# First loads in halves, one weight piece later in the queue, and signs folded into other operations, in a retention and feed-forward kernel

## The chip, the cores and the metric

The kernel runs on one core of a Trainium2 chip. The metric is the device time of one execution in microseconds. Engines are named as in the profile: PE (TensorE; PEld is its weight load), DVE (VectorE), ACT (ScalarE), POOL (GpSimd) and SP (SyncE, whose queue issues the loads and stores; SPq).

## The reference, cut to what matters

Three stages follow each other. Retention over 4 batches, 8 heads, 576 tokens and head size 64; a product of two projections with two more matrices behind it; and a projection with a leaky activation whose slopes are alpha. Inputs of the later stages are float64 weights.

```
scores = q @ k.T / sqrt(64)                 # q, k, v: (4, 8, 576, 64)
ret    = scores * gamma[h] ** (i - j)       # for i >= j, else 0
x      = (ret @ v) as (2304, 512)
h      = ((x @ w1) * (x @ w2)) @ w3         # w1, w2: (512, 1024)
x      = h @ w_out                          # (2304, 512)
g      = max(x @ w_in, 0) + alpha * min(x @ w_in, 0)     # alpha: (2048,)
out    = g @ w_out2                         # (2304, 512)
```

## The kernel before

**Retention** (class Retention) works on chunks of 128 tokens, four and a half of them in a batch, and on pairs of heads; a batch has 4 pairs. For chunk c, `scores(c)` multiplies k and q on PE (L419; L408 for the last, half chunk) and has DVE multiply by the mask into rt (L423, L411); `moments(c)` multiplies k and v (L434) and has DVE and POOL build the running state (L440 to L446); `values(c)` multiplies the state of the chunk before by q (L467) and v by rt (L476), and ACT and DVE split the result into a high and a low part for the next product (L181, L182). q is scaled first by POOL (`scale`, L396 for the 512 full columns and L398 for the 64 last), k by ACT (`prep`, L389, one instruction for each head). A batch is stepped by `steps()`: scores and moments of the next chunk around values of this one.

Batch 0 is done in two halves, r0 (pairs 0 and 1) and r1 (pairs 2 and 3). Ahead of it, `busy(26)` lets PE run 26 matmuls on zeros (L575), and each of r0's first steps ends with one more (`keep_busy`). `ready(2)` and `ready(3)` scale and prepare one pair of r1 each.

**Weights** come in pieces of 512 KB as float64 bits (raw) and are turned into two float32r halves in four steps: `_first` (ACT, L93 and L94), `_second` (DVE, L103 to L108), `_third` (ACT, L114), `_fourth` (DVE, L122). `tick` moves each step by one piece; it also loads ahead, `self.near` pieces beyond the one begun. Pieces 0 and 1 are needed by the first unit of the first product (`ab_unit(0, 0)`), pieces 2 and 3 by the next.

**The first product** is made in units (`ab_unit`, PE L188: 12 matmuls for each half), with retention of batch 1, 2 and 3 put between them a step at a time by `cycle`. A half's result is copied by ACT (L651), multiplied by DVE (L641), split by ACT and DVE (L637, L633) and stored (L630). After the first half of the first unit, `cycle` first ticks the weights (which runs `_third` of piece 2 and then `_first` of piece 3), then flushes what is waiting (L651), then runs the first step of batch 1: scaling and preparing its pairs 0 and 1.

**The order of the loads.** PE, SP and ACT work in the order of the program; DVE's and POOL's order is made by the scheduler from its own estimates. The loads stand in SP's queue as: the row constants, the table (mask, its tail, and the scale of q) of pairs 0 and 1, then q and k, then kv of pairs 0 and 1; weight piece 0; the same for pairs 2 and 3; pieces 1 to 3; pairs 2 and 3 of batch 1 in room of their own (`load_apart`); piece 4; pairs 0 and 1 of batch 1; piece 5 and on.

**The operands of the last product** (class Operands) are made from w_out2 in pairs of pieces x, y, five pairs between 120 and 212 us (the case without `small`) and three later, with `small`, on POOL. For each, `signed` multiplies both pieces by the signs sg of alpha (L309 on DVE; L307 on POOL), `less` makes sums and differences (L290), and `hi` and `lo` split them (L271 on ACT, L275 on DVE).

Of the kernel before, what the change touches and what calls it, by code (L numbers as in the profile page):

```python
# [32 lines left out]
def _f32(ap):  # L33
    return ap.bitcast(F32)
# [112 lines left out]
def retention_moe_kernel(ctx: ExitStack, tc, qk, kv, w_out1, w3t, w12, w_in, w_out2, alpha, c_row, c_pair, out):  # L147
# [11 lines left out]


    al = const.tile([P, 96], F32, name="al")
    al, sg, sal = (al[:, n * C2:(n + 1) * C2] for n in range(3))
    const_r = pool(ctx, "const_r", side="right")
    const_r.tile([P, 120], F32, name="pad")

# [61 lines left out]
    class Operands:  # L227
# [40 lines left out]
        def hi(self, j, u, src):  # L268
            self.u[j, u] = self.places(j, u)
            for h, _, x in self.halves(j, u, src):  # L270
                nc.scalar.copy(h, x)  # L271

        def lo(self, j, u, src):
            for h, l, x in self.halves(j, u, src):
                nc.vector.tensor_tensor(out=l, in0=x, in1=_f32(h), op=ALU.subtract)  # L275
            t = self.u.pop((j, u))
            if j != self.stays:
                for n, op in enumerate(self.PLACES[u]):
                    nc.sync.dma_start(out=wod[WOPS.index(op)][:, j].rearrange("p (h w) -> p h w", h=2),
                                      in_=_f32(t[:, n]))  # L280

        def add(self, j, at, steps, ahead=None):


            w, x, y = self.w, 2 * j, 2 * j + 1
            lower, upper = slice(0, 256), slice(256, 512)
            t = {}

            def less(out, a, b):
                (nc.gpsimd if self.small else nc.vector).tensor_tensor(out=out, in0=a, in1=b, op=ALU.subtract)  # L290

            def sums1():
                a, b = w.ab[x][0], w.ab[y][0]
                t[1] = tmp.tile([P, 512], I32, tag="b", name=f"t1_{j}", bufs=2).bitcast(F32)
                less(t[1][:, lower], a[:, upper], a[:, lower])
                less(t[1][:, upper], b[:, upper], t[1][:, lower])

            def sums3():
                a, b = w.ab[x][0], w.ab[y][0]
                t[3] = tmp.tile([P, 512], I32, tag="b", name=f"t3_{j}", bufs=2).bitcast(F32)  # L300
                less(t[3][:, lower], b[:, upper], a[:, upper])
                less(t[3][:, upper], b[:, lower], t[1][:, upper])

            def signed(i):
                a = w.ab[i][0]
                if self.small:
                    nc.gpsimd.tensor_tensor(out=a, in0=a, in1=sg[:, i:i + 1].to_broadcast([P, 512]), op=ALU.mult)  # L307
                else:
                    nc.vector.tensor_scalar(out=a, in0=a, scalar1=sg[:, i:i + 1], scalar2=None, op0=ALU.mult)  # L309

            parts = {
                "gx": lambda: signed(x), "gy": lambda: signed(y),
                "fx": lambda: w._first(x), "fy": lambda: w._first(y),
                "sx": lambda: w._second(x), "sy": lambda: w._second(y),
                "h1": lambda: self.hi(j, "u1", w.ab[x][0][:, lower]),
                "l1": lambda: self.lo(j, "u1", w.ab[x][0][:, lower]),
                "h2": lambda: self.hi(j, "u2", w.ab[y][0]), "l2": lambda: self.lo(j, "u2", w.ab[y][0]),
                "t1": sums1, "t3": sums3,
                "h3": lambda: self.hi(j, "u3", t[1]), "l3": lambda: self.lo(j, "u3", t[1]),
                "h4": lambda: self.hi(j, "u4", t[3]), "l4": lambda: self.lo(j, "u4", t[3]),  # L320
                "x": lambda: self.load(x + 2), "y": lambda: self.load(y + 2),
            }
# [48 lines left out]
    class Retention:  # L371
# [20 lines left out]
        def scale(self, pairs=None):  # L392
            for p in pairs or self.pairs:
                q, by = qt[self.b][p], qs[:, p]
                full = q[:, 0:512].rearrange("p (c i) -> p c i", i=CH)
                nc.gpsimd.tensor_tensor(out=full, in0=full, in1=by.unsqueeze(1).to_broadcast([P, 4, CH]),  # L396
                                        op=ALU.mult)
                nc.gpsimd.tensor_tensor(out=q[:, 512:S], in0=q[:, 512:S], in1=by[:, 0:64], op=ALU.mult)  # L398

        def scores(self, c):  # L400
            b, n = self.b, self.n
# [168 lines left out]
    load_apart(1, 3, 13)  # L570
    warm = pool(first, "ps_warm", space=PSUM).tile([P, 512], F32, name="warm")
# [8 lines left out]
    r0.scale()  # L580
    r0.prep()

    def keep_busy(step):
        def run():
            step()
            flush()
            busy(1)
        return run

    def ready(p):  # L590
        def run():
            r1.scale([p])
            r1.prep([p])
# [896 lines left out]
```

## Time and profile before

| | |
|---|---|
| median of 3 runs | 780.6 us (779.77 to 782.58) |
| profiled execution | 783.55 us |
| its span, first to last instruction | 781.7 us |
| mean granted clock of PE | 0.997 |
| PE busy | 768.9 us, 98% |
| DVE busy | 587.3 us, 75% |
| ACT busy | 380.4 us, 49% |
| POOL busy | 63.8 us, 8% |

The profile comes from one execution. PE is busy nearly throughout, so the places where it isn't are to be looked for one by one; a busy share is a mean over stages that differ.

### The profile page before, as it was taken

Reading aid. Unit: us, or ns where it says so; the run is one execution under the profiler, and the core shown is the slowest. Engines: PE = TensorE matmul, PEld = TensorE weight load, DVE = VectorE, ACT = ScalarE, POOL = GpSimd, SP = SyncE. Lnnn points to the kernel's source line nnn. Section 1 sums busy time; section 2 is a strip of 40 time slices with the busy share of each in tenths; the row PEclk is TensorE's granted clock in tenths of the full one; section 3 lists DMA queues with packets and bytes.
Section 4 is the critical chain, followed back from the end, with each engine's and each line's share of the span. In section 5 each row is a group of like instructions: output and inputs, shape, how many; then the busy total and the mean of one; then the engine's idle time right before and its main releaser. Section 6 shows DMA issues by size and latency. Waiting matters only on the chain.

```text
span 781.7 us, 13197 instructions
## 1 busy us (share of the span) xinstructions
PE 768.9 (98%) x4928; PEld 688.9 (88%) x4928; DVE 587.3 (75%) x951; ACT 380.4 (49%) x665; POOL 63.8 (8%) x73
## 2 busy tenths in 40 slices
PE   8999999998999999999999999999999999999998
PEld 5788788887788988899999999999999888888887
DVE  4894889569857779688974768778767877777874
ACT  3643474334445466464654546546534444444442
POOL 4410400051000000000000200110200000000000
PEclk9999999999999999999999999999999999999999
DMA  9943965798576667799993796564899754444440
GB/s 353 358 160 105 340 246 202 239 287 259 212 249 204 189 197 256 248 327 368 407 375 138 262 362 225 172 228 154 286 339 366 234 152 128 140 126 136 135 128 28
DMA packets 116225, 182.11 MB, mean 233 GB/s; under 512 B 9920, under 2 KB 82624, under 8 KB 116160
## 3 DMA queue, kind: packets, MB, share of 16 engines
q1 hardware_dynamic: 116160, 181.26, 68.1%
q8 instruction: 39, 0.64, 0.4%
q14 instruction: 26, 0.21, 0.1%
HBM read 117.00 MB, written 64.23 MB: 232 GB/s over the span
## 4 chain that ended last, share of the span: by engine, by line
PE 83%; DVE 7%; DMA 5%; issue 2%; SPq 2%; ACT 1%; POOL 0%; DVEq 0%; ACTq 0%; POOLq 0%
PE h L1063 21%; PE ps L188 19%; PE y L1007 13%; PE o L1208 12%; PE o L1210 6%; PE pw L822 6%; DMA abd<-ab 2%; PE sc L419 2%; PE o L476 2%; DMA cells<-gd 2%; DVE cells L1189 2%; PE o L467 1%; SPq L514 1%; PE st L434 1%; DVE a L108 1%
## 5 line engine op out<-in xcount | busy, mean ns | idle before, releaser
L188 PE MATMUL ps<-xh,w 128*128 128x512 f32 (+1 forms) x640 | 186.1, 372 | 1.8 <-ACT f L651 1.8
L188 PEld LDWEIGHTS ps<-xh,w 128*128 128x128 f32 x640 | 116.1, 188 | 23.3 <-ACT f L651 2.2
L1208 PE MATMUL o<-wop,cells 128*128 128x512 f32 x504 | 126.4, 393 | 0.9 <-DVE cells L1220 0.9
L188 PE MATMUL ps<-xl,w 128*128 128x512 f32 (+1 forms) x320 | 118.0, 369 | 0.0
L1208 PEld LDWEIGHTS o<-wop,cells 128*128 128x128 f32 x504 | 90.8, 189 | 17.7 <-issue 1.4
L1007 PE MATMUL y<-yab,wp 128*128 128x384 f32 x576 | 100.0, 334 | 0.0
L1007 PEld LDWEIGHTS y<-yab,wp 128*128 128x128 f32 x576 | 99.9, 188 | 0.1
L1189 DVE TENSOR_TENSOR cells<-cells,cells 128x1024 fp32r<-128x1024 f32 x63 | 76.4, 1222 | 25.7 <-ACT cells L1183 25.6
L1210 PEld LDWEIGHTS o<-wop,cells 128*128 128x128 f32 x504 | 68.7, 190 | 4.9
L1210 PE MATMUL o<-wop,cells 128*128 128x256 f32 x504 | 70.2, 282 | 0.0
L188 PEld LDWEIGHTS ps<-xl,w 128*128 128x128 f32 x320 | 60.4, 189 | 9.5
L1183 ACT CAST cells<-cells 128x1024 fp32r<-128x1024 f32 x63 | 64.9, 1054 | 7.0 <-DVE cells L1176 4.6
L108 DVE CUSTOM_DVE_ANT_0 a<-a,b 128x1024 uint16<-128x1024 uint16 x72 | 53.2, 738 | 2.9
L1063 PE MATMUL h<-xT,wu 128*128 128x384 f32 x288 | 54.7, 334 | 0.2 <-DVE g L1082 0.2
L1063 PE MATMUL h<-xT,wv 128*128 128x384 f32 x288 | 54.9, 335 | 0.0
L1076 DVE SCALAR_TENSOR_TENSOR g<-h,al,g 128x384 f32<-128x384 f32 x48 | 29.4, 614 | 32.6 <-ACT g L1075 29.5
L637 ACT CAST ab<-f 128x512 fp32r<-128x512 f32 (+1 forms) x40 | 23.1, 577 | 61.2 <-DVE f L641 51.8
L1063 PEld LDWEIGHTS h<-xT,wu 128*128 128x128 f32 x288 | 50.3, 188 | 0.5 <-DVE g L1082 0.5
L1063 PEld LDWEIGHTS h<-xT,wv 128*128 128x128 f32 x288 | 50.3, 188 | 0.3 <-DVE g L1082 0.3
L103 DVE TENSOR_SCALAR a<-a 128x512 f32<-128x512 f32 x72 | 31.9, 443 | 22.9 <-ACT a L93 22.5
L822 PE MATMUL pw<-wo,w 128*128 128x512 f32 x192 | 43.7, 389 | 0.0
L822 PEld LDWEIGHTS pw<-wo,w 128*128 128x128 f32 x192 | 36.0, 188 | 7.4
(130 smaller groups left out, 1139.4 us busy)
## 6 DMA issues: line engine op xcount, KB each, us to landing
gd<-g SPq DMA_DIRECT2D x96, 192.0 KB, 4.4
cells<-gd SPq DMA_DIRECT2D x36, 512.0 KB, 6.3
abd<-ab SPq DMA_DIRECT2D x32, 512.0 KB, 5.2
wod<-wo2u SPq DMA_DIRECT2D x49, 256.0 KB, 4.0
wop<-wod SPq DMA_DIRECT2D x21, 512.0 KB, 6.5
yab<-abd SPq DMA_DIRECT2D x24, 384.0 KB, 8.0
raw<-in_w_dram SPq DMA_DIRECT2D x16, 512.0 KB, 8.0
rawo<-in_w_out_dram SPq DMA_DIRECT2D x16, 512.0 KB, 5.2
```

Source lines behind the costliest of these rows:

```text
L103: nc.vector.tensor_scalar(out=a, in0=a, scalar1=self.LEAST, scalar2=self.MOST, op0=ALU.max, op1=ALU.min)
L108: nc.vector.tensor_tensor(out=a.bitcast(I32), in0=a.bitcast(I32), in1=b, op=ALU.add)
L188: nc.tensor.matmul(ps, a, bb, start=(n == 0), stop=(n == last))
L637: nc.scalar.copy(t[:, 0], f)
L822: nc.tensor.matmul(acc[i], a[:, ic], bb, start=(k == 0 and n == 0), stop=(k == C1 - 1 and n == 2))
L1007: nc.tensor.matmul(ys[o], wpc[c][a][:, oc], yab[b, c][:, bb], start=(c == 0 and i == 0), stop=(c == C1 - 1 and i == 2))
L1063: nc.tensor.matmul(ps, a[:, x, ks], b[:, y, k], start=(fresh and n == 0), stop=(n == 5), skip_group_check=True)
L1076: nc.vector.scalar_tensor_tensor(out=g, in0=ps, scalar=sal[:, c], in1=g, op0=ALU.mult, op1=ALU.max)
L1183: nc.scalar.copy(h.bitcast(F32R), self.q[name])
L1189: nc.vector.tensor_tensor(out=l.bitcast(F32R), in0=q[name], in1=h, op=ALU.subtract)
L1208: nc.tensor.matmul(ps, h[:, k], w[k], start=(fresh and k == 0), stop=(k == C1 - 1), skip_group_check=True)
L1210: nc.tensor.matmul(ps[:, 256:], l[:, k], w[k][:, 0:256], start=False, stop=(k == C1 - 1), skip_group_check=True)
```

## The change

Five things change. (1) Batch 0's q, k and kv are loaded by halves: chunks 0 and 1 of both pairs first (with the scale of q ahead of them and the masks behind them), then the rest; scaling and preparing follow the same halves, and r0's first two steps are written out as `begun` and `second`. (2) 18 dummies instead of 26 stand ahead, and two instead of one behind each of the four kept-busy steps. (3) `ready(2)` and `ready(3)` prepare both pairs of r1, first their first halves, then the rest. (4) Only weight pieces 0 to 2 are loaded ahead; piece 3 and then piece 4 follow behind pairs 0 and 1 of batch 1 (`near` is 0 up to `loads`, then 4). (5) In the early operands of w_out2, the multiplication by the sign is dropped; the splits and differences take the sign as a scalar, and a table of the products of two signs, `both`, is made beside sg. The operands made later, on POOL, stay as they are.

```diff
-    al, sg, sal = (al[:, n * C2:(n + 1) * C2] for n in range(3))
+    al, sg, sal, both = (al[:, n * C2:(n + 1) * C2] for n in range(4))
+    both = both[:, 0:C1]
...
+                if sign is None:
+                    nc.scalar.copy(h, x)
+                else:
+                    nc.scalar.activation(h, x, AF.Copy, scale=sign)
...
+                if sign is None:
+                    nc.vector.tensor_tensor(out=l, in0=x, in1=_f32(h), op=ALU.subtract)
+                else:
+                    nc.vector.scalar_tensor_tensor(out=l, in0=x, scalar=sign, in1=_f32(h), op0=ALU.mult,
+                                                   op1=ALU.subtract)
...
-                else:
-                    nc.vector.tensor_scalar(out=a, in0=a, scalar1=sg[:, i:i + 1], scalar2=None, op0=ALU.mult)
...
-        def prep(self, pairs=None):
+        def prep(self, pairs=None, chunks=slice(0, 4)):
...
-                    nc.scalar.activation(k[:, 4 * j:4 * j + 4], k[:, 4 * j:4 * j + 4], AF.Copy,
-                                         scale=kd[:, 2 * p + j:2 * p + j + 1])
+                    x = k[:, 4 * j + chunks.start:4 * j + chunks.stop]
+                    nc.scalar.activation(x, x, AF.Copy, scale=kd[:, 2 * p + j:2 * p + j + 1])
...
-    nc.sync.dma_start(out=per_pair[:, 0:2], in_=c_pair[:, 0:2])
-    load_pair(0, 0)
-    load_pair(0, 1)
+    def load_qk(p, cols):
+        nc.sync.dma_start(out=first_x[p][:, :, cols], in_=qk[0, p, :, :, cols])
+
+    def load_kv(p, chunks):
+        y, src = (z[:, 0:16].rearrange("p (g c) d -> p g (c d)", g=4)[:, :, chunks.start * D:chunks.stop * D]
+                  for z in (first_y[p], kv[0, p]))
+        nc.sync.dma_start(out=y, in_=src)
...
+        load_table(pairs, slice(2 * CH + 64, 3 * CH + 64))
+        for p in pairs:
+            load_qk(p, slice(0, 2 * CH))
+        for p in pairs:
+            load_kv(p, begin)
+        load_table(pairs, slice(0, 2 * CH + 64))
+
+    def load_rest(pairs):
+        for p in pairs:
+            load_qk(p, slice(2 * CH, S))
+            load_kv(p, rest)
+            nc.sync.dma_start(out=first_y[p][:, 16], in_=kv[0, p, :, 16])
+
+    load_begin((0, 1))
+    load_rest((0, 1))
     ws.load_until(1)
-    nc.sync.dma_start(out=per_pair[:, 2:4], in_=c_pair[:, 2:4])
-    load_pair(0, 2)
-    load_pair(0, 3)
-    ws.load_until(4)
+    load_begin((2, 3))
+    load_rest((2, 3))
+    ws.load_until(3)
+    ws.near = 0
     load_apart(1, 2, 10)
     load_apart(1, 3, 13)
...
-    busy(26)
+    busy(18)
...
-            busy(1)
+            busy(2)
...
+    def begun():
+        r0.scores(0)
+        r0.scores(1)
+        flush()
+        r0.moments(0)
+        r0.scale(None, rest)
+
+    def second():
+        flush()
+        r0.values(0)
+        r0.moments(1)
+        r0.prep(None, rest)
+
     def loads():
         load_pair(1, 0)
         load_pair(1, 1)
+        ws.near = 4
...
-    for step in (b(s0[0]), b(s0[1]), one, b(s0[2]), one, b(s0[3]), ready(2), one, s0[4], ready(3), one, s1[0],
+    for step in (b(begun), b(second), one, b(s0[2]), one, b(s0[3]), ready(2), one, s0[4], ready(3), one, s1[0],
...
+    pairs = sg.rearrange("p (j r) -> p j r", r=2)
+    nc.vector.tensor_tensor(out=both, in0=pairs[:, :, 0], in1=pairs[:, :, 1], op=ALU.mult)
```

## Rows read from the trace of the kernel before

**Rows 1.** The page, busy time of each engine.
```profile
PE 768.9 (98%) x4928; PEld 688.9 (88%) x4928; DVE 587.3 (75%) x951; ACT 380.4 (49%) x665; POOL 63.8 (8%) x73
```
**Rows 2.** Timeline of the start: start, duration, engine, work, idle before and releaser.
```profile
1.45 7.57 PE L575 MATMUL warm<-idle 128*128 128x512 bf16 x26 [1.45 <-DVE idle L167]
...
5.20 3.33 PEld L575 LDWEIGHTS <-idle 128*128 128x128 bf16 x16 [0.20 <-issue]
...
6.45 1.27 POOL L396 TENSOR_TENSOR qk<-qk,per_pair 128x512 f32<-128x512 f32 x1 [6.00 <-DMA qk<-in_qk_dram]
...
10.38 0.91 ACT L389 ACTIVATE kv<-kv,per_row 128x256 f32<-128x256 f32 x2 [1.70 <-DMA kv<-in_kv_dram]
...
10.45 0.49 PE L419 MATMUL sc<-qk 64*128 64x128 f32 x4 [1.00 <-POOL qk L396]
```
**Rows 3.** Timeline around 36 us, where batch 1 begins.
```profile
34.12 1.30 POOL L396 TENSOR_TENSOR qk<-qk,per_pair 128x512 f32<-128x512 f32 x1 [0.26 <-DMA qk<-in_qk_dram]
...
34.24 0.67 ACT L93 ACTIVATE a<-raw 128x512 f32<-128x512 f32 x1
...
35.36 0.57 ACT L651 COPY f<-ps 128x512 f32<-128x512 f32 x1
...
35.83 1.71 ACT L389 ACTIVATE kv<-kv,per_row 128x256 f32<-128x256 f32 x4
...
38.08 0.50 PE L188 MATMUL ps<-xh,w 128*128 128x512 f32 x1
```
**Rows 4.** Table of stretches: busy time by engine, clock, DMA share, GB/s.
```profile
10.00:20.00 10.00, 9.53 (x130) 7.04 (x132) 7.66 (x17) 4.53 (x11) 5.78 (x9) 1.00 1.02 418
...
685.00:687.00 2.00, 2.00 (x12) 1.67 (x11) 1.52 (x2) 1.54 (x2) 0.00 (x0) 1.00 1.15 341
...
598.00:620.00 22.00, 22.00 (x128) 19.54 (x127) 15.08 (x19) 8.40 (x11) 0.00 (x0) 1.00 0.94 302
```
**Rows 5.** Loads of the first 37 us: size of each and time to landing.
```profile
raw<-in_w_dram SPq DMA_DIRECT2D x7, 512.0 KB, 9.3
qk<-in_qk_dram SPq DMA_DIRECT2D x6, 576.0 KB, 7.2
kv<-in_kv_dram SPq DMA_DIRECT2D x6, 544.0 KB, 7.8
...
per_pair<-const_pair_dram SPq DMA_DIRECT2D x2, 448.0 KB, 6.1
```
**Rows 6.** Table of stretches around two gaps of PE.
```profile
94.00:96.00 2.00, 0.66 (x3) 0.57 (x4) 1.17 (x2) 1.81 (x4) 0.00 (x0) 1.00 1.03 424
...
182.00:184.00 2.00, 1.30 (x12) 1.30 (x14) 2.00 (x5) 0.57 (x2) 0.54 (x1) 0.65 1.03 405
184.00:186.00 2.00, 2.00 (x20) 1.78 (x20) 2.00 (x5) 0.18 (x1) 1.66 (x1) 0.50 1.00 399
```
**Rows 7.** The chain that ended last, in order of time: start, duration, work.
```profile
184.78 1.64 PE o L476 x16
...
192.55 1.09 PE sc L419 x16
...
194.24 1.02 PE o L476 x16
```
**Rows 8.** VectorE's groups by shape, 160 to 212 us: busy, mean ns.
```profile
L275 DVE TENSOR_TENSOR wo2u<-t,wo2u 128x512 fp32r<-128x512 f32 x4 | 2.7, 683 | 2.1 <-ACT wo2u L271 2.1
```
**Rows 9.** Timeline at 95 us, and of 171 to 183 us.
```profile
95.34 0.50 PE L188 MATMUL ps<-xh,w 128*128 128x512 f32 x1 [1.75 <-ACT f L651]
...
171.74 0.47 DVE L309 TENSOR_SCALAR a<-a,al 128x512 f32<-128x512 f32 x1
...
172.13 0.68 DVE L106 SCALAR_TENSOR_TENSOR a<-rawo,a 128x512 uint32<-128x512 uint32 x1
...
181.43 1.21 DVE L423 TENSOR_TENSOR rt<-sc,per_pair 128x1024 f32<-128x1024 f32 x1
...
182.70 2.08 PE L419 MATMUL sc<-qk 64*128 64x128 f32 x16 [2.38 <-DVE rt L423]
```

More of the change, by code (lines that the diff above doesn't have):

```diff
@@ L266, in halves, with hi, lo @@
             return [(t[:, :, 0], t[:, :, 1], src)]
-        def hi(self, j, u, src):
+        def hi(self, j, u, src, sign=None):
             self.u[j, u] = self.places(j, u)
             for h, _, x in self.halves(j, u, src):
-                nc.scalar.copy(h, x)
-        def lo(self, j, u, src):
-            for h, l, x in self.halves(j, u, src):
-                nc.vector.tensor_tensor(out=l, in0=x, in1=_f32(h), op=ALU.subtract)
+                if sign is None:
+                    nc.scalar.copy(h, x)
+                else:
+                    nc.scalar.activation(h, x, AF.Copy, scale=sign)
+        def lo(self, j, u, src, sign=None):
+            for h, l, x in self.halves(j, u, src):
+                if sign is None:
[3 more added lines that the diff above has]
+                                                   op1=ALU.subtract)
             t = self.u.pop((j, u))
@@ L287, in add, with less @@
             t = {}
-            def less(out, a, b):
-                (nc.gpsimd if self.small else nc.vector).tensor_tensor(out=out, in0=a, in1=b, op=ALU.subtract)
+            late = not self.small
+            sx, sy, sxy = (sg[:, x:x + 1], sg[:, y:y + 1], both[:, j:j + 1]) if late else (None, None, None)
+            def less(out, a, b, sign=None):
+                if sign is not None:
+                    nc.vector.scalar_tensor_tensor(out=out, in0=a, scalar=sign, in1=b, op0=ALU.mult, op1=ALU.subtract)
+                else:
+                    (nc.gpsimd if self.small else nc.vector).tensor_tensor(out=out, in0=a, in1=b, op=ALU.subtract)
             def sums1():
@@ L295, in sums1 @@
                 less(t[1][:, lower], a[:, upper], a[:, lower])
-                less(t[1][:, upper], b[:, upper], t[1][:, lower])
+                less(t[1][:, upper], b[:, upper], t[1][:, lower], sxy)
             def sums3():
@@ L300, in sums3 @@
                 t[3] = tmp.tile([P, 512], I32, tag="b", name=f"t3_{j}", bufs=2).bitcast(F32)
-                less(t[3][:, lower], b[:, upper], a[:, upper])
-                less(t[3][:, upper], b[:, lower], t[1][:, upper])
+                less(t[3][:, lower], b[:, upper], a[:, upper], sxy)
+                less(t[3][:, upper], b[:, lower], t[1][:, upper], sxy)
             def signed(i):
                 a = w.ab[i][0]
-                if self.small:
+                if not late:
                     nc.gpsimd.tensor_tensor(out=a, in0=a, in1=sg[:, i:i + 1].to_broadcast([P, 512]), op=ALU.mult)
-                else:
-                    nc.vector.tensor_scalar(out=a, in0=a, scalar1=sg[:, i:i + 1], scalar2=None, op0=ALU.mult)
             parts = {
@@ L388, in prep, with scale @@
                 for j in range(2):
-                    nc.scalar.activation(k[:, 4 * j:4 * j + 4], k[:, 4 * j:4 * j + 4], AF.Copy,
-                                         scale=kd[:, 2 * p + j:2 * p + j + 1])
-        def scale(self, pairs=None):
+                    x = k[:, 4 * j + chunks.start:4 * j + chunks.stop]
+                    nc.scalar.activation(x, x, AF.Copy, scale=kd[:, 2 * p + j:2 * p + j + 1])
+        def scale(self, pairs=None, chunks=slice(0, 4)):
             for p in pairs or self.pairs:
                 q, by = qt[self.b][p], qs[:, p]
[L395 to L398, printed above, removed]
+                full = q[:, chunks.start * CH:chunks.stop * CH].rearrange("p (c i) -> p c i", i=CH)
+                nc.gpsimd.tensor_tensor(out=full, in0=full, in1=by.unsqueeze(1)
+                                        .to_broadcast([P, chunks.stop - chunks.start, CH]), op=ALU.mult)
+                if chunks.stop == 4:
+                    nc.gpsimd.tensor_tensor(out=q[:, 512:S], in0=q[:, 512:S], in1=by[:, 0:64], op=ALU.mult)
         def scores(self, c):
@@ L575, in busy @@
             nc.tensor.matmul(warm, idle[:, 0:P], idle[:, :512], start=True, stop=True)
-    busy(26)
+    busy(18)
     r0, r1 = Retention(0, [0, 1], psum0), Retention(0, [2, 3], psum0)
     s0, s1 = r0.steps(), r1.steps()
-    r0.scale()
-    r0.prep()
+    for p in r0.pairs:
+        r0.scale([p], begin)
+    for p in r0.pairs:
+        r0.prep([p], begin)
     def keep_busy(step):
@@ L591, in run @@
         def run():
-            r1.scale([p])
-            r1.prep([p])
-        return run
+            if p == 2:
+                r1.scale(None, begin)
+                r1.prep(None, begin)
+            else:
+                r1.scale(None, rest)
+                r1.prep(None, rest)
+        return run
+    def begun():
[9 more added lines that the diff above has]
+        r0.prep(None, rest)
     def loads():
```

20 lines of the change are left out of this document (15 added, 5 removed).

## Prediction

> **What bounds the kernel now.** I read the page's busy shares first: TensorE is busy 98% of the span [rows 1], so a change pays only where TensorE stands still, and I looked for those places with the table of stretches and the waits of TensorE. Up to 220 us there are four: the start, a stretch around 36 us, a gap of 1.75 us that ends at 95.34, and one of 2.38 us that ends at 182.70 [rows 9]. The change touches the first two by its loads and the last by its signs. Then I read the timeline around each and asked which release came last.
>
> *The start.* Twenty-six dummies hold TensorE from 1.45 for 7.57 us, and the second pair's scores run only at 10.45, as they wait for GpSimd's scaling of q, which waits for the load [rows 2]. From there TensorE runs nearly without a break through both halves of batch 0 and into the first units of the next product.
>
> *Around 36 us.* TensorE's order is fixed: two units, then scores(0) of batch 1, moments(0), the third unit. Scores(0) needs GpSimd's scaling of pair 1 of batch 1, which starts at 34.12 when its q and k have landed. Moments(0) needs ScalarE's four scalings of k (35.83 to 37.54), and the third unit starts right behind it, at 38.08. ScalarE works in order, too: the scalings stand behind the copy L651 (35.36), which stands behind L93 and L94 of the fourth weight piece (from 34.24) [rows 3]. So whatever is late at L93 of the fourth piece is late at the third unit, one for one, and everything after it on TensorE starts from there.
>
> *The loads.* All loads go through one queue in the order of the program, and from 10 to 20 us, as an example, the 16 DMA engines are full: share 1.02, 418 GB/s [rows 4]. When a load lands is therefore the bytes ahead of it, not when it is issued.
>
> **The change, part by part.**
>
> *Halves of the first batch.* Each first load of q and k shrinks from 576 to 256 KB, and the scaling waits for 128 KB of table instead of 448 [rows 5]. Nine dummies run until 5.2 us and 17 from there to 9.02 (0.22 us each), so 18 end at 5.2 + 9 x 0.22 = 7.2 us. By then both pairs' halves have landed and are scaled: the load of 1,030 KB (6 + 448 + 576) was there at 6.45 [rows 2]; the first two halves of q and k are 646 KB with their table, about 1 us sooner at 387 KB per us (worked out below), and GpSimd's two halves take 0.65 us each (half of 1.27). The second pair's scores move from 10.45 to 7.2, 3.25 us sooner. Against it, four more dummies go between the steps (0.22 each): 0.9 us. So TensorE may be 2.4 us earlier in this stretch. The last parts of the second two pairs, whose scaling ScalarE must do before it goes on, land no earlier than now, so some of the 2.4 may be lost there; I keep 0 to 2.4 us and show that it does not matter. Batch 0 takes 24 loads instead of 10. The fourteen more issues stand on SP's queue, which has the time as long as the DMA engines behind it stay full; if they did not, everything below would land later still. GpSimd and ScalarE run twice as many instructions of half the size, and both wait for loads here, which covers what that costs them.
>
> *The order of the loads behind it.* The pieces up to q and k of pair 1 of batch 1 add up, from the sizes [rows 5], to 6 + 2 x 448 + 4 x (576 + 544) for batch 0, 5 x 512 for weights, 2 x (576 + 544) for the two pairs loaded apart (in other cuts), and 576 + 544 + 576: 11,878 KB, landed at 34.1 [rows 3]. The first batch's two pairs (2,694 KB) had landed when ScalarE took the second k at 10.38 [rows 2]. That is 9,184 KB in 23.7 us, 387 KB per us. After the change the fourth weight piece comes behind all of batch 1's loads, the fifth behind it: ahead of its end stand 11,878 - 512 + 544 = 11,910 KB. At the same rate it lands at 34.2 us. ScalarE needs it at 34.24 now. So the earlier start is worth nothing at this gate even if the halves cost no bandwidth: what TensorE gains before 33 us it spends waiting at 36 us. Today piece four has long landed then.
>
> *The halves cost bandwidth.* A partition's row of kv (4,352 bytes) is now four pieces of 512 bytes, twice, and a tail; q and k are two of 1,024 and two of 1,280; the table two and two. Counted over two pairs that is 3,840 pieces instead of 640, so 6,400 more for the batch. The trace has no load of just this form at the start. The nearest are the reads of cells in 512-byte pieces: 341 GB/s with the DMA engines full [rows 4], 1.50 ns for a piece. A 4,352-byte row at 418 GB/s takes 10.4 ns. The line through both has 0.31 ns for each piece besides its bytes; 6,400 x 0.31 = 2.0 us. Bounds: 0, if a piece costs only its bytes; 3.4 us, if I take 302 GB/s from a longer, mixed stretch (598 to 620) instead. I take 2.0, as the full stretch is cleaner. Piece four then lands at 36.2, 2.0 us after ScalarE has it now. L93, L94, L651 and the scalings follow at the old spacing, the last moments at 39.6, the third unit at 40.1: +2.0 us. Pair 1's q and k land at 34.1 - 2.6 + 2.0 = 33.5 and are scaled by 35, so scores(0) stands where it stood.
>
> The Trainium skill ("DMA: Bandwidth & Descriptors", Specifications) puts line rate at transfers of 512 bytes and up. By it these pieces would cost nearly nothing, and this term would be about 0 instead of 2.0. The 341 against 418 GB/s of this trace speaks against it.
>
> *The clock behind that wait.* TensorE would stand from scores(0) (done about 36.3) to the first moments (about 38.9), 2.6 us, and mostly before it as well. After 2.38 us idle at 182.7 the granted clock was 0.65 and 0.50 in the next two stretches, the lower level of 1.2 GHz; after 1.75 us at 95.3 it stayed 1.00 [rows 6, 9]. The dip made 16 scores 2.08 us instead of 1.09 and 16 value matmuls 1.64 instead of 1.02 [rows 7, 9]: 1.6 us. Bounds here 0 and 1.6; as 2.6 is above 2.38, I take 1.6.
>
> *The fewer dummies* cost nothing themselves: real work follows at once. *The table of products of signs* is one more VectorE operation, on 128x8 elements, long before its first reader; it is smaller than any in the rows, so I bound it by 0 and the 0.39 us of an operation on 128x512 [rows 9], and take 0, as VectorE has slack there.
>
> *Signs as scalars.* Ten VectorE multiplications L309 vanish (0.47 us each [rows 9]). The subtractions that take the sign instead change from a two-operand form to one with a scalar: at 128x512 these take 683 ns (L275 [rows 8]) and 0.68 us (L106 [rows 9]), so they cost the same. ScalarE's copies become scalings of the same size, off the path. Most of the ten are hidden: VectorE has slack. At 181.43 it has none: mask L423 starts behind a full queue, scores wait for it until 182.70, and two L309 stand ahead of it in that queue, the first at 171.74 with the next operation 0.39 us behind its start [rows 9]. Without them L423 starts 0.8 us sooner, the gap falls from 2.38 to 1.6, below the 1.75 that left the clock alone, so the 1.6 us of the dip go, too: -2.4 us. Bounds: 0, as VectorE's order is made anew by the planner and may put other work there; -2.4.
>
> **Sum.** +2.0 (piece four) + 1.6 (clock behind it) - 0.8 - 1.6 (gap at 182) = +1.2 us. The profiled execution took 783.55 us, span 781.7 and 1.85 around it; it becomes 784.75. The median of the runs is 780.6, 2.95 below; the same difference gives 781.8, and I say 782.
>
> **Rivals.**
> *The pieces cost only their bytes.* Piece four lands at 34.2, the front stays as it is (0) and the gap at 182 gives its 2.4: 778.2; 780 if the clock dips without that. For it: these loads all read inputs, unlike cells; against it: 341 GB/s. The line-rate rule of the Trainium skill ("DMA: Bandwidth & Descriptors", Specifications) is this case.
> *ScalarE does not meet the wait.* If piece four lands by 31.8, or if its conversion runs after the scalings, the 2.4 of the start come through: -2.4 - 2.4 = -4.8, 775.8. Against it: the byte count, which would have to be 900 KB smaller, and ScalarE's fixed order.
> *VectorE's new order puts the mask no earlier* (slower). At 181 us two more operations of a conversion, at the 0.68 us of L106 [rows 9], may come ahead of L423, as any operation there is planned, not written. From 0.8 us of such work on, the saving is gone; with 1.4 the gap grows by 0.6 to 3.0 and the dip stays: +2.0 + 1.6 + 0.6 = +4.2, 784.8. For it: VectorE is busy for all of 182 to 186 us, too [rows 6]; against it: two operations less.
>
> **How the numbers follow.** Forecast 0.42 (its own range 779.5 to 784.5); only bytes 0.20; no wait 0.13; mask no earlier 0.25. A measurement tells 0.5%, 3.9 us: 776.7 to 784.5. Faster: the third case and a little of the second, 0.15. Slower: most of the fourth and the forecast with 3.4 us of piece cost, 0.24. Same: 0.61. The range for 8 in 10 leaves out half of the third case and the far end of the fourth: 776 to 786.5.
>
> **What would show it.** Dummies end near 7.2; scores(2) and the first batch's end come 1 to 2.4 us sooner. L93's fourth instance starts near 36 with a wait for the load of raw; before the last moments TensorE stands over 2 us and the granted clock falls; the third unit starts near 40 instead of 38.08. DMA rate in the first 20 us is below 400 GB/s. L309 is gone at 120 to 210, and the scores that start at 182.70 now wait under 1.75 us at full clock. It is wrong if L93 of piece four starts before 34 us, or if the rate of the first 20 us stays at 418.

## The result, and the profile after

The changed kernel takes 785.4 us (median of 20 runs, 783.1 to 791.8) against 781.0 us of the kernel before (20 runs, 779.0 to 785.6): ratio 1.0054, interval 1.0037 to 1.0072. It is slower by 4.4 us, half a per cent. The prediction was 782: the time lies inside its range of 776 to 786.5, which is wide, and 0.9 us above the forecast's own range (779.5 to 784.5). Of its three cases "slower" (0.24) came in, by a hair: 0.54% where the line was 0.5%, with the interval on both sides of it. The execution that was profiled is a long one: 790.0 us, span 788.2, mean granted clock 0.994. It lies 4.6 us above its median, that of before 2.5 above its own, so positions are read from it and totals from the medians.

The page shows the same division of work as [rows 1]: VectorE is one microsecond less busy, ScalarE three more.

```profile
PE 771.7 (98%) x4924; PEld 689.6 (87%) x4924; DVE 586.3 (74%) x942; ACT 383.7 (49%) x673; POOL 63.1 (8%) x77
```

The timeline of the start, to be held against [rows 2] (kernel lines have moved: L396 is now L411, L419 L435, L389 L405, L188 L189):

```profile
1.45 5.54 PE L623 MATMUL warm<-idle 128*128 128x512 bf16 x18 [1.45 <-DVE idle L168]
...
5.17 1.40 POOL L411 TENSOR_TENSOR qk<-qk,per_pair 128x256 f32<-128x256 f32 x2 [4.73 <-DMA qk<-in_qk_dram]
...
6.92 1.16 PE L435 MATMUL sc<-qk 64*128 64x128 f32 x16
...
10.66 0.73 POOL L411 TENSOR_TENSOR qk<-qk,per_pair 128x256 f32<-128x256 f32 x1 [4.09 <-DMA qk<-in_qk_dram]
...
12.32 0.72 POOL L411 TENSOR_TENSOR qk<-qk,per_pair 128x256 f32<-128x256 f32 x1 [0.66 <-DMA qk<-in_qk_dram]
...
31.45 0.50 PE L189 MATMUL ps<-xh,w 128*128 128x512 f32 x1
```

The dummies end at 6.99 and both pairs' scores run at 6.92, as forecast. But the second halves of q and k land only at 10.6 and 12.3, and the first unit of the product starts at 31.45. In the kernel before it started at 30.17:

```profile
30.17 0.50 PE L188 MATMUL ps<-xh,w 128*128 128x512 f32 x1
```

The lead of the start is gone by then and 1.3 us more.

The table of stretches says where (us, then busy time of PE, PEld, DVE, ACT and POOL, the granted clock, DMA share, GB/s):

```profile
2.00:8.00 6.00, 6.00 (x34) 2.73 (x32) 0.00 (x0) 0.20 (x2) 1.40 (x2) 1.00 0.84 229
8.00:24.00 16.00, 14.37 (x186) 9.62 (x184) 8.65 (x21) 8.61 (x25) 8.12 (x14) 1.00 1.07 355
```

The same two rows of the kernel before:

```profile
2.00:8.00 6.00, 6.00 (x22) 2.33 (x21) 0.00 (x0) 0.44 (x3) 1.54 (x2) 1.00 0.96 343
8.00:24.00 16.00, 14.91 (x201) 10.88 (x199) 10.62 (x24) 7.20 (x18) 7.20 (x11) 1.00 1.03 417
```

Two losses are to be seen, of different kinds. From 2 to 8 us the DMA engines are less busy (0.84) and move 114 GB/s less: 6 x 114 = 684 KB behind, 1.65 us at 415 KB per us. (By steps of 2 us their share is 0.58, 1.08 and 0.85 there: low at the ends of the stretch, full in the middle.) From 8 to 24 us they are full (1.07) and still move 62 GB/s less: 16 x 62 = 992 KB, 2.4 us. Together 4.05 us.

The timeline around the beginning of batch 1, against [rows 3]:

```profile
35.68 1.29 POOL L411 TENSOR_TENSOR qk<-qk,per_pair 128x512 f32<-128x512 f32 x1 [0.47 <-DMA qk<-in_qk_dram]
...
38.19 0.67 ACT L93 ACTIVATE a<-raw 128x512 f32<-128x512 f32 x1 [2.52 <-DMA raw<-in_w_dram]
...
39.32 0.56 ACT L719 COPY f<-ps 128x512 f32<-128x512 f32 x1
...
39.79 1.70 ACT L405 ACTIVATE kv<-kv,per_row 128x256 f32<-128x256 f32 x4
...
40.34 1.47 PE L450 MATMUL st<-kv 128*64 128x64 f32 x7 [2.07 <-ACT kv L405]
...
42.03 0.79 PE L189 MATMUL ps<-xh,w 128*128 128x512 f32 x1
```

This is the forecast chain, each step in its place: ScalarE stands 2.52 us for the fourth weight piece, which lands at 38.19 and not at 36.2; the copy and the four scalings stand behind L93 and L94; TensorE stands 2.07 us for the first scaling. The third unit starts at 42.03, 3.95 us after 38.08. And the clock falls behind the wait, to 0.51, the lower of its two levels:

```profile
42.00:44.00 2.00, 2.00 (x7) 1.58 (x6) 2.00 (x5) 2.00 (x5) 0.66 (x1) 0.51 0.70 164
44.00:46.00 2.00, 2.00 (x7) 1.59 (x6) 2.00 (x5) 0.83 (x2) 0.00 (x0) 0.64 0.89 356
```

The third unit's twelve matmuls take 4.5 us there instead of 3.0, so in this execution the dip costs 1.5.

Further on, the unit behind the gap that ended at 95.34 [rows 9] starts at 101.91. It waits for ScalarE, which waits for the store of the result three units earlier (ab has three buffers); SyncE issued that store at 91.67 instead of 85.66, behind the loads of batch 2. So this gap doesn't take up the delay: the loads whose buffers TensorE frees move with it.

### The profile page after: what moved, and what is told of

It reads as the page before. It is cut to its first block, busy times and chain, and to the rows that moved or that the text cites. A ratio compares the mean times of both kernels' runs of the same rounds, so it can differ in the third digit from the quotient of the medians.

```text
span 788.2 us, 13212 instructions
## 1 busy us (share of the span) xinstructions
PE 771.7 (98%) x4924; PEld 689.6 (87%) x4924; DVE 586.3 (74%) x942; ACT 383.7 (49%) x673; POOL 63.1 (8%) x77
## 4 chain that ended last, share of the span: by engine, by line
PE 88%; DMA 7%; DVE 2%; SPq 1%; issue 1%; ACT 1%; POOL 0%; ACTq 0%; DVEq 0%; POOLq 0%
PE h L1133 22%; PE ps L189 19%; PE o L1278 15%; PE y L1077 13%; PE o L1280 8%; PE pw L892 6%; DMA qk<-in_qk_dram 4%; DMA raw<-in_w_dram 2%; PE o L492 2%; PE sc L435 1%; DMA abd<-ab 1%; PE o L483 1%; PE st L450 1%; DVE a L106 0%; SPq L585 0%
## 5 line engine op out<-in xcount | busy, mean ns | idle before, releaser
L189 PE MATMUL ps<-xh,w 128*128 128x512 f32 (+1 forms) x640 | 189.1, 377 | 2.8 <-ACT f L719 2.8
L189 PEld LDWEIGHTS ps<-xh,w 128*128 128x128 f32 x640 | 118.0, 191 | 25.1 <-ACT f L719 3.3
L189 PE MATMUL ps<-xl,w 128*128 128x512 f32 (+1 forms) x320 | 119.5, 373 | 0.0
L189 PEld LDWEIGHTS ps<-xl,w 128*128 128x128 f32 x320 | 61.4, 192 | 9.8
```

The lines of the kernel that those rows point to most:

```text
L189: nc.tensor.matmul(ps, a, bb, start=(n == 0), stop=(n == last))
```

## The experiments

In short: the median of the runs, its ratio to the kernel before with the interval, the start of L93 of the fourth piece, of the third unit and of the unit behind the gap near 95 us, each from one profiled execution. Runs of one kernel spread over 4 to 10 us, and the kernel before had medians of 781.0 to 782.4 beside these runs, so the ratios count. Under "clock" stands the mean granted clock over a kernel's runs, for the kernel before over the 98 that ran beside them. Under "rest" stands the mean time less what the clock took of it, (1 - clock) x span; this is an estimate.

```
kernel                  us     ratio  interval         clock   rest   L93    third  at 95
before                 781.0   -      -                0.9977  780.4  34.24  38.08   95.34
changed                785.4   1.0054 1.0037 to 1.0072 0.9966  783.3  38.19  42.03  101.91
1 signs alone          780.7   0.999  0.997  to 1.0011 0.9992  780.7  34.40  38.23   96.75
2 front, old signs     787.6   1.0084 1.0051 to 1.0116 0.9957  784.1  37.62  41.46   99.66
3 piece moved alone    781.7   0.9999 0.9976 to 1.0021 0.9990  781.0  34.81  38.66   94.78
4 halves, piece ahead  783.8   1.003  1.0013 to 1.0047 0.9994  783.6  35.40  40.63   98.62
5 dense halves         784.5   1.0025 0.9999 to 1.005  0.9965  781.9  35.89  39.74   98.14
6 first step late      782.8   0.9998 0.9977 to 1.0019 0.9991  782.1  38.39  39.12   97.41
7 kv by 512 bytes      783.9   1.0013 0.9987 to 1.004  0.9968  781.5  33.55  38.30   97.28
8 kv by 2,048 bytes    782.6   0.9986 0.9959 to 1.0014 0.9979  780.7  37.22  41.07   97.36
9 q and k alone cut    784.6   1.0038 1.0014 to 1.0062 0.9959  780.9  36.53  40.37   96.38
10 second two whole    788.2   1.0078 1.0049 to 1.0107 0.9945  783.3  36.77  40.60   99.81
11 whole, step late    781.5   1.0    0.9979 to 1.0022 0.9984  781.0  37.20  38.14   95.50
12 dense, step late    782.3   1.0007 0.9986 to 1.0028 0.9982  781.0  35.93  36.77   96.90
```

**Which part costs: runs 1 to 4.** Run 1 is the kernel before with the hunks on the signs alone.

> The kernel before with the signs as scalars and nothing else of the change. Theory A (the front loses: the fourth weight piece lands late and ScalarE waits for it in its order): nothing of the front is here, so the third unit starts at 38.1 as before; VectorE saves ten multiplications of 0.48 us but each of the 35 rewritten operations takes about 0.07 us longer (0.75 against 0.68 at 128x512 in the changed kernel), so the time is 0 to 2.4 us shorter, about 1. Theory B (the signs make the kernel slower, as the scalar form and VectorE's new order cost more than the multiplications): 3 to 4 us longer than before.

Run 2 is the changed kernel with the old signs:

```diff
-            late = not self.small
+            late = False
...
-                if not late:
+                if self.small:
                     nc.gpsimd.tensor_tensor(out=a, in0=a, in1=sg[:, i:i + 1].to_broadcast([P, 512]), op=ALU.mult)
+                else:
+                    nc.vector.tensor_scalar(out=a, in0=a, scalar1=sg[:, i:i + 1], scalar2=None, op0=ALU.mult)
```

> The changed kernel with the signs as they were before. Theory A: all of the loss is here; the fourth piece lands at 38.2, the third unit starts at 42.0, the clock falls behind it, and the time is 4 to 5.5 us longer than before. Theory B: no difference from before within 1 us.

Run 3 is the kernel before with the fourth piece behind the second batch:

```diff
-    ws.load_until(4)
+    ws.load_until(3)
+    ws.near = 0
...
         load_pair(1, 1)
+        ws.near = 4
```

> The kernel before, with only the fourth and fifth weight pieces behind the loads of batch 1; loads whole. Theory A says that lateness is bytes ahead plus what small pieces cost: without them the fourth piece lands at 34.2, ScalarE begins it at 34.3 as now, the third unit starts at 38.1 (within 0.3), the time is within 0.7 us of before. Rival C (the order alone is at fault, the halves are not): the fourth piece lands after 36, the third unit starts at 40 or later, and the time is 3 us or more longer.

Run 4 is the changed kernel with the opposite edit: halves, but the fourth piece ahead.

> The changed kernel with the fourth and fifth weight pieces back ahead of batch 1's loads; halves and signs stay. Theory A: the wait moves and does not go: ScalarE finds its piece, but q and k of pair 1 land 2.6 us later than in the changed kernel (35.7 + 2.6 = 38.3) and its kv at 39.5, so scores(0) starts at 39.6 and the third unit at 41.3, 0.7 us sooner than in the changed kernel at best; 3 to 4.5 us longer than before. Rival C (the order alone is at fault): back to the time of before or better, third unit at 38 or sooner.

Signs alone change nothing that can be told (0.999); the front alone has the whole loss (1.0084 over six runs, and 1.0054 with the signs). Moving the piece alone costs nothing: in run 3 it is there when ScalarE comes to it, without a wait for a load:

```profile
34.81 0.67 ACT L93 ACTIVATE a<-raw 128x512 f32<-128x512 f32 x1
```

With halves and the piece ahead (run 4) the wait is not gone, it moves to the loads that the piece is now in front of:

```profile
35.40 0.67 ACT L93 ACTIVATE a<-raw 128x512 f32<-128x512 f32 x1
...
37.82 1.28 POOL L411 TENSOR_TENSOR qk<-qk,per_pair 128x512 f32<-128x512 f32 x1 [0.65 <-DMA qk<-in_qk_dram]
...
39.03 0.91 ACT L405 ACTIVATE kv<-kv,per_row 128x256 f32<-128x256 f32 x2 [1.11 <-DMA kv<-in_kv_dram]
...
40.63 0.50 PE L189 MATMUL ps<-xh,w 128*128 128x512 f32 x1
```

1.4 us come back, since kv then lacks only two scalings; the time is 0.3% longer than before, 2.3 us, where 3 to 4.5 had been expected. So the lateness belongs to the loads, and the order decides who meets it.

In run 1 the gap that ended at 182.70 [rows 9] is 0.72 us, and the clock holds, as forecast:

```profile
181.67 1.21 DVE L437 TENSOR_TENSOR rt<-sc,per_pair 128x1024 f32<-128x1024 f32 x1
...
182.93 1.16 PE L433 MATMUL sc<-qk 64*128 64x128 f32 x16 [0.72 <-DVE rt L437]
...
184.00:186.00 2.00, 2.00 (x36) 1.87 (x35) 2.00 (x5) 0.00 (x0) 2.00 (x1) 1.00 1.04 413
```

But the multiplication by the mask starts no sooner, at 181.67 instead of 181.43: TensorE comes to the gap 1.9 us later (182.21 instead of 180.32), 1.3 of it from the gap near 95, which is 3.05 us in this execution instead of 1.75. The other kernels say more. In runs 4 to 6 and 10 to 12, all with the signs as scalars, this gap is 0.7 to 1.8 us and the clock is 1.00 from 184 to 190. In the kernel before and in runs 3, 7 and 9, with the old signs, it is 2.4 to 2.5 and the clock 0.72 to 0.83 there; in runs 2 and 8, old signs too, it is 1.55 and the clock 1.00.

**Why the loads are late: runs 5 and 7 to 10.** In run 5 the two halves of a partition's rows lie one behind the other in DRAM, so that a half is one run of a partition instead of two or four pieces; the reads of the tiles follow. The core of it:

```diff
-        nc.sync.dma_start(out=first_x[p][:, :, cols], in_=qk[0, p, :, :, cols])
+        nc.sync.dma_start(out=first_x[p][:, cols], in_=qk[0, p].rearrange("p a s -> p (a s)")[:, cols])
...
-        nc.sync.dma_start(out=y, in_=src)
+        rows = slice(0, 8) if chunks is begin else slice(8, 17)
+        nc.sync.dma_start(out=first_y[p][:, rows], in_=kv[0, p, :, rows])
```

> The changed kernel with the same halves in the same order, but q, k and kv of batch 0 laid out so that a half is one piece in each partition (1 to 2.5 KB instead of 512 bytes to 1.3 KB): 3,072 pieces instead of 7,680, 20 loads instead of 24. Theory A (small pieces cost bandwidth): the changed kernel's fourth piece came 4.0 us after the 34.2 of the byte count, 0.62 ns for each of 6,400 pieces; 1,792 cost 1.1, so it lands at 35.3, the third unit starts at 39.2 instead of 42.0, and the time is 0 to 1.5 us longer than before. Rival D (many small loads, each with its issue and its landing, starve the DMA engines; the size of a piece does not matter): the fourth piece lands after 37.5, third unit after 41, 3 us or more longer than before.

```profile
2.00:8.00 6.00, 6.00 (x20) 2.10 (x20) 0.00 (x0) 0.81 (x4) 1.45 (x2) 1.00 0.87 258
8.00:24.00 16.00, 15.33 (x214) 10.79 (x216) 11.46 (x26) 9.27 (x26) 7.58 (x14) 1.00 1.04 407
```

From 8 to 24 us the rate is nearly back: 10 GB/s short of before instead of 62, 0.4 us instead of 2.4. So the pieces, and the longer issues that go with them, were worth 2.0 us there. (In run 2, with the same loads as the changed kernel, the rate of that stretch is 374, a loss of 1.7: the size differs from execution to execution.) From 2 to 8 us it is still 85 GB/s short, 1.2 us: that part did not go with the pieces. L93 starts at 35.89, 0.6 later than expected, and the time is 2.0 us longer than before, where 0 to 1.5 had been expected; in that the expectation was too good.

Runs 7 and 8 take the kernel before and cut only kv of batch 0, by the same number of loads, once across the chunks (pieces of 512 bytes), once along the row (2,048):

```diff
+            if b == 0:
+                for half in (slice(0, 128), slice(128, 256)):
+                    nc.sync.dma_start(out=y[:, 0:16].rearrange("p (g c) d -> p g (c d)", g=4)[:, :, half],
+                                      in_=kv[b, p, :, 0:16].rearrange("p (g c) d -> p g (c d)", g=4)[:, :, half])
+                nc.sync.dma_start(out=y[:, 16], in_=kv[b, p, :, 16])
+                return
```

> The kernel before, order kept, with batch 0's kv loaded as two loads of four 512-byte pieces in each partition and the tail in a third: 4,096 pieces more, 8 loads more, the same bytes. Theory A: at 0.62 ns a piece, q and k of pair 1 of batch 1 land 2.5 us later, at 36.6 instead of 34.1; the third unit starts about 40 and the time is 1.5 to 3.5 us longer. Rival D (the number of loads): as x8, which has as many loads.

> As x7, the same 8 loads more with the same bytes, but each half as one piece of 2,048 bytes: 1,024 pieces more. Theory A: 0.6 us later, at 34.7; third unit within 0.8 us of 38.1; the time within 1 us of before. Rival D: the same lateness as x7.

The stretch in which most of the cut kv is on its way, run 7 and then run 8:

```profile
14.00:20.00 6.00, 6.00 (x91) 4.56 (x90) 5.55 (x14) 3.08 (x7) 4.69 (x6) 1.00 1.11 380
```

```profile
14.00:20.00 6.00, 6.00 (x82) 4.57 (x78) 5.03 (x11) 1.92 (x5) 3.52 (x5) 0.86 1.05 411
```

With as many loads and the engines full in both, the stretch moves 380 GB/s with 512-byte pieces and 411 with 2,048-byte pieces (415 before). In run 7 1,960 of its 2,618 packets are such pieces, 1.0 of its 2.28 MB; so the pieces alone went slower than 380. Pair 1 of batch 1 is scaled from 35.29 in run 7 and from 34.74 in run 8, against 34.12: +1.2 and +0.6. Run 7 was expected at +2.5, so a piece of kv costs about half of what I had then concluded from the changed kernel. (In run 8's execution the third unit starts at 41.07 for another reason: the second pair's scores run at 11.29 instead of 10.45, the clock falls to 0.57 behind that wait, the first unit starts at 32.03 instead of 30.17, and a step of VectorE before the fourth piece is late with it. The time over all its runs is no longer for it.)

Run 9 cuts q and k instead:

```diff
-            nc.sync.dma_start(out=x, in_=qk[b, p])
+            if b == 0:
+                for cols in (slice(0, 256), slice(256, S)):
+                    nc.sync.dma_start(out=x[:, :, cols], in_=qk[b, p, :, :, cols])
+            else:
+                nc.sync.dma_start(out=x, in_=qk[b, p])
```

> The kernel before, with q and k of the first batch alone loaded in two halves of their columns: 4 loads more, 1,536 pieces more, now of 1,024 and 1,280 bytes instead of 2,304; kv stays whole. If every piece costs alike (0.2 to 0.3 ns, as the 512-byte and 2,048-byte cuts of kv gave), q and k of pair 1 of batch 1 come 0.3 to 0.5 us later than in the kernel before: their scaling starts at 34.5 to 34.6 instead of 34.12, and the time stays within 0.3% of before. Rival: it is these cuts of q and k, two runs in a partition to a piece pair, that fill the DMA engines without bytes; then the scaling starts at 35.5 or later, and the rate of 8 to 20 us falls below 390 GB/s.

(Whole, q and k come in one piece of 4,608 bytes for each partition, 576 KB over 128.) Neither theory has it right. The scaling starts at 36.01 (+1.9), which the rival gave, but its mechanism isn't there: from 8 to 20 us the rate is 407 GB/s. Two thirds of the bytes that are missing by 24 us are missing by 8, where 288 GB/s were moved instead of 343. All that is missing by 24 us is 1.1 us of the 1.9; the rest I can't account for. SyncE's issues at the start show a difference; first of the kernel before, then of run 9 (two issues in its row):

```profile
1.65 0.42 SPq L534 DMA_DIRECT2D qk<-in_qk_dram  x1
```

```profile
1.65 1.29 SPq L536 DMA_DIRECT2D qk<-in_qk_dram  x2
```

A pair's 576 KB take SyncE 0.42 us whole and 1.29 in two halves, and SyncE issues without a break there. In the changed kernel it hands out the first two pairs and their tables, 2,688 KB, from 1.19 to 9.36 instead of 1.18 to 3.75. That the DMA engines lacked work by it is not shown: by 7.5 us 2.1 MB were issued there, and by 8 us 1.4 MB had moved.

The time of run 9 is 0.4% longer, most of it at the clock (rest 780.9). In its profiled execution the third unit is not late by a load at the gate: the second pair's scores wait at the start, the clock is 0.50 from 14 to 16 us, the first unit starts at 32.47, and what ScalarE waits for ahead of L93 is VectorE:

```profile
11.81 0.49 PE L419 MATMUL sc<-qk 64*128 64x128 f32 x4 [1.40 <-POOL qk L396]
...
36.00 0.62 ACT L114 CAST w<-a 128x512 fp32r<-128x512 f32 x1 [1.54 <-DVE a L108]
```

Run 10 is the changed kernel with the second two pairs whole again:

```diff
-    load_begin((2, 3))
-    load_rest((2, 3))
+    nc.sync.dma_start(out=per_pair[:, 2:4], in_=c_pair[:, 2:4])
+    load_pair(0, 2)
+    load_pair(0, 3)
...
-            if p == 2:
-                r1.scale(None, begin)
-                r1.prep(None, begin)
-            else:
-                r1.scale(None, rest)
-                r1.prep(None, rest)
+            r1.scale([p])
+            r1.prep([p])
```

> The changed kernel, but pairs 2 and 3 of batch 0 loaded and scaled whole as before; only pairs 0 and 1 come in halves. 3,200 pieces fewer than the changed kernel, 7 loads fewer. If the pieces alone made the loads late, half of the lateness of about 4 us goes: the fourth weight piece lands near 36.2, the third unit starts near 40.0. If 1.65 us of it are the first 8 us, in which small loads did not fill the DMA engines, those stay and only half of the other 2.4 us goes: the piece lands near 37.0, the third unit near 40.9. The time between those of before and after in both, 782.5 to 784.5.

```profile
2.00:8.00 6.00, 6.00 (x25) 2.39 (x24) 0.00 (x0) 0.21 (x2) 1.40 (x2) 1.00 0.79 220
...
14.00:20.00 6.00, 5.27 (x75) 3.43 (x72) 5.00 (x11) 3.38 (x8) 2.81 (x4) 1.00 1.02 418
```

The loss of the first 8 us stays whole (220 against 229) and behind the cut loads the rate is that of before at once: the third unit at 40.60 is near the 40.9 of the theory with two losses, away from 40.0. The time is a miss: 788.2, above both kernels that it lies between. What it has more is at the clock: its mean granted clock is the lowest of all, 0.9945, and without the clock's share it takes 783.3 us, as the changed kernel does. Where the clock falls is not shown, as the profiled execution (784.2 us, clock 0.999) is one of the few in which it hardly does.

**Whose order makes lateness a stall: runs 6, 11, 12.** Run 6 leaves all loads of the changed kernel as they are and puts the first step of a weight piece (L93, L94) behind the copies and scalings that are ready at that point:

```diff
-    def tick(self, upto=None):
+    def tick(self, upto=None, only=(3, 2, 1, 0)):
...
-        for n in (3, 2, 1, 0):
+        for n in only:
...
-                ws.tick(upto)
+                ws.tick(upto, (3, 2, 1))
                 flush()
                 r.tick(rate)
+                ws.tick(upto, (0,))
```

> The changed kernel with one thing moved on ScalarE: the first step of a weight piece (L93, L94) goes behind the copy and the scalings of batch 1 instead of ahead of them. Theory A (the price is ScalarE's order: the scalings stand behind a wait for a load that they do not need): the wait for the fourth piece no longer holds moments(0); pair 1's kv lands about 37.0 and is scaled by 38, the third unit starts at 38.5 instead of 42.0 and the clock does not fall, so 3 to 4 us of the loss are back; some 1 us may return at the fourth unit, which needs that piece. Rival E (batch 1's own loads are as late as the piece): third unit at 40.5 or later, less than 1.5 us back.

```profile
37.17 0.91 ACT L405 ACTIVATE kv<-kv,per_row 128x256 f32<-128x256 f32 x2 [0.15 <-DMA kv<-in_kv_dram]
...
38.39 0.69 ACT L93 ACTIVATE a<-raw 128x512 f32<-128x512 f32 x1 [0.31 <-DMA raw<-in_w_dram]
...
39.12 0.50 PE L189 MATMUL ps<-xh,w 128*128 128x512 f32 x1
...
46.76 0.50 PE L189 MATMUL ps<-xh,w 128*128 128x512 f32 x1 [1.34 <-DVE w L122]
```

The piece lands as late as in the changed kernel (38.39), and the third unit comes 2.9 us sooner, with no dip. The loss in time is gone: 0.9998 instead of 1.0054. Of the 3.2 us between the mean times of the two kernels some 2.0 are at the clock (0.9991 instead of 0.9966) and 1.2 in the rest; of the rest 1.7 us stay against the kernel before. What is late next is the conversion of that piece: inside the fourth unit TensorE waits 1.34 us for its weights.

Runs 11 and 12 were to beat both kernels: run 11 has the first batch whole, signs, moved piece and the late step; run 12 the same with dense halves.

> The kernel before with the signs as scalars, the fourth weight piece behind the second batch, and the first step of a weight piece put behind the copies and scalings of the unit on ScalarE; the first batch loaded whole, 26 dummies. A candidate to beat both. If ScalarE's order at the late piece is what the moments wait for, the scalings need not wait for L93 any more: the third unit at 37.6 to 38.1, the gap near 182 us under 1.75 us at full clock, and the time 0 to 2 us below that of before (ratio 0.997 to 1.000). Rival: the conversion of piece four, put later, comes late at VectorE and at the fourth unit instead: the time 0 to 2 us above before.

> The changed kernel with both remedies: the halves lie whole in DRAM, so that each is one run of each partition, and the first step of a weight piece stands behind the scalings on ScalarE. Dense halves left 1.3 to 1.5 us of lateness, all of it from the first 8 us; with ScalarE's order mended the scalings wait for kv of batch 1 alone, so the third unit starts at 38.0 to 38.5, and with the signs the time comes out within 1.5 us of before (ratio 0.998 to 1.002). If the halves gave what the earlier start at 7.2 promised, the third unit would be at 37 or sooner and the ratio 0.997 or less.

Neither does: 1.000 and 1.0007. Run 12 shows it best. The halves give at last what they promised, the first unit at 29.41 instead of 30.17 and the third at 36.77 instead of 38.08. TensorE then spends it in two waits:

```profile
44.39 0.72 PE L189 MATMUL ps<-xh,w 128*128 128x512 f32 x2 [1.33 <-DVE w L122]
...
96.90 0.50 PE L189 MATMUL ps<-xh,w 128*128 128x512 f32 x1 [3.05 <-ACT f L729]
```

1.3 us won at 37 are gone at 44 in the wait for the same piece's conversion, and near 95 the unit starts 1.6 us later than before. Run 11 wins nothing at all at 38 us: its first unit starts at 30.72 and TensorE itself is the bound there.

## Why the prediction was right or wrong

*The chain around 36 us* was right in every step: late piece, ScalarE in order, moments, third unit, clock. Run 6 shows that it is the order: with the same late piece and another order the stall is gone. The move without the halves costs nothing (run 3). How far a late third unit reaches the end was taken as one for one; the changed kernel's 3.95 us are some 2.9 there (783.3 against 780.4 without the clock).

*The term of the fourth piece* was mis-sized: 2.0 us, measured 3.95 at the third unit. It had one loss where there are two. The pieces were priced at 2.0 us; the rate from 8 to 24 us gives 2.4 (1.7 in run 2), of which dense halves take back 2.0 (run 5): about right. What was missing is the start: 1.65 us up to 8 us. The prediction had its condition in words ("if they did not, everything below would land later still"), and cost fourteen issues at nothing because "the DMA engines behind it stay full". They were not full (0.84). Run 5 and run 10 keep this loss while they take the other away. Whether SyncE's issuing causes it is not settled: the 0.64 us for each cut load speak for it, but dense halves are issued faster (0.47) and lose 1.2 us there all the same, and issued bytes were waiting; no run changed the queue alone. The sign that was to show the term, a rate below 400 GB/s in the first 20 us, was badly put: the kernel before moves 354 there itself. From 8 to 20 us it is 348 against 419.

*The start*, priced at 0 to 2.4 us sooner, was 1.3 us late by the first unit, for the same reason: the second halves came late. That it would not matter at the gate held, but by another course than I gave.

*The clock* was right in the profiled execution: 1.6 forecast, 1.5 measured. Over all runs the changed kernel loses only some 0.9 us more at the clock than the kernel before. And the dip is absent in run 2 behind a wait of 1.86 us and present in run 5 behind one of 1.11, first run 2, then run 5:

```profile
39.77 1.47 PE L452 MATMUL st<-kv 128*64 128x64 f32 x7 [1.86 <-ACT kv L407]
...
42.00:44.00 2.00, 2.00 (x10) 1.64 (x9) 2.00 (x5) 2.00 (x5) 0.66 (x1) 1.00 0.85 240
```

```profile
38.05 1.47 PE L462 MATMUL st<-kv 128*64 128x64 f32 x7 [1.11 <-ACT kv L415]
...
40.00:42.00 2.00, 2.00 (x7) 1.56 (x7) 1.97 (x6) 1.89 (x4) 0.26 (x1) 0.63 0.31 66
```

So the length of that wait alone, by which I chose, does not decide it.

*Signs*: a shorter gap at full clock came about in run 1, 0.72 us where 1.6 was forecast, and in the other kernels with signs where no late load stood in the way. That the mask starts 0.8 us sooner did not. The 2.4 us do not show in the time: 0.999, interval 0.997 to 1.0011, that is 2.3 us less to 0.9 more. One reason: the 1.6 us of the dip were read from one profiled execution of 783.55 us, but in 39 of the 98 executions of the kernel before the mean granted clock is 0.999 or more (median 780.4 us), and those have no dip of that size to lose. Against the 29 executions beside it, run 1 loses 1.3 us less at the clock, and the rest of its time is no shorter. In the profiled execution of the changed kernel this gap has another cause: late loads of batch 3 stop the scores for 1.56 us, and the clock falls to 0.50. The equal price of the scalar form was wrong by 0.06 us (below): of the 4.8 us of the ten L309, 2.3 go back into subtractions over that stage.

*The sum*: +3.95 + 1.5 - (0 to 2.4) = 3.1 to 5.5, measured 4.4; forecast 1.2. That the time fell inside the stated range owes more to its width than to the sum, which was 3.2 us short. Of the rivals, "only bytes" falls by run 7 against run 8. The Trainium skill ("DMA: Bandwidth & Descriptors", Specifications) gives 512 bytes as the least transfer for line rate. This trace does not agree: 380 GB/s where 44% of the bytes come in pieces of 512, 411 with pieces of 2,048, with full engines. "ScalarE does not meet the wait" is what run 6 made true by hand, but without the 4.8 us that this rival promised. Of "mask no earlier" the start came about in run 1 (181.67), but not the longer gap and the dip that it priced.

## What to carry to other kernels

Before a first load is split to start sooner, sum up what its queue hands out: here two halves took the issuing engine longer than the whole, the start moved a third fewer bytes, and whatever stood behind them in the queue was late, at a gate 30 us further on. Where an in-order engine does work for two consumers, put the work that waits for a late load behind the work whose data is there; with the halves kept, that took the whole half per cent away here, where dense halves left 0.25% (interval 0 to 0.5). Before a clock dip is priced from one profile, look at how many executions have it. And time won ahead of a stage counts only up to the next wait: 1.3 us won at 37 us were spent at 44.

## What the runs showed of the hardware

VectorE's subtraction with a scalar factor is not the price of the two-operand form. Groups by shape, before and after, same stage (count, busy us, mean ns of one):

```profile
L275 DVE TENSOR_TENSOR wo2u<-t,wo2u 128x512 fp32r<-128x512 f32 x9 | 6.2, 685 | 4.6 <-ACT wo2u L271 4.6
```

```profile
L283 DVE SCALAR_TENSOR_TENSOR wo2u<-t,al,wo2u 128x512 fp32r<-128x512 f32 x10 | 8.2, 824 | 6.1 <-ACT wo2u L276 6.1
...
L283 DVE SCALAR_TENSOR_TENSOR wo2u<-a,al,wo2u 128x512 fp32r<-128x512 f32 x5 | 3.8, 755 | 1.4 <-ACT wo2u L276 1.4
```

The mean of 824 ns holds one instruction of 1.52 us, which ran while GpSimd was busy:

```profile
185.04 1.48 POOL L400 TENSOR_TENSOR kv<-kv,per_row 128x512 f32<-128x512 f32 x1
...
185.55 1.52 DVE L283 SCALAR_TENSOR_TENSOR wo2u<-t,al,wo2u 128x512 fp32r<-128x512 f32 x1
```

Without it 685 ns become about 750 (run 1: 744 and 742), and ScalarE's scaled copy of the same size takes 722 where the plain copy took 623.

A busy share near 1 says little of the rate: the 16 DMA engines moved 355 GB/s at a share of 1.07 in the changed kernel and 417 at 1.03 before.
